# Feed-forward products that read their moving columns in turn from the two halves of a tile

## The chip, the cores and the metric

One Trainium2 chip, one of its cores. The metric is the device time of one execution in microseconds (us); lower is better. The kernel before takes 1040.09 us, the median of three runs from 1039.26 to 1040.59.

## What is computed

The kernel computes linear attention followed by a feed-forward network. The attention (8 batches, 8 heads, 576 tokens, head dimension 64, 128 features) makes the rows `x` of 4608 tokens by 512 features; the network then is

```python
h = x @ w_in                                            # 4608 x 512 times 512 x 2048
g = np.maximum(h, 0.0) + alpha * np.minimum(h, 0.0)     # a leaky relu with a slope for each of the 2048
return (g @ w_out).astype(np.float32)                   # 4608 x 2048 times 2048 x 512
```

Inputs and outputs are float32.

## The kernel before

**Layout.** Tokens lie along the free dimension everywhere in the feed-forward: a tile holds 128 features by 512 tokens, and the output leaves as 512 features by 4608 tokens, which the host transposes. The tokens are nine chunks of 512 (`NC2`, `C2`). The stationary operand of a matmul is a 128x128 block of weights; the moving operand is one tile of 512 columns; the result is one bank of PSUM with 512 columns.

**Three matmuls for one product.** Every operand of the feed-forward is split into a high part, rounded to the type fp32r, and the rest (`rnd` at L139 on ScalarE, `low` at L143 on VectorE). A product of two blocks is three matmuls that add into one bank: high weight by high tokens, low weight by high tokens, high weight by low tokens. They are written out in `gemm1` (L538 to L545), `gemm2` (L550 to L554) and `three` (L828 to L831). The trace shows these operands as f32.

**Stages.** First the attention, 32 pairs of heads, with float32 matmuls: projections (L347), sums of keys and values (L387), denominators (L470, four matmuls that each fill 32 output partitions and read four different moving operands), transposes (L430, L433) and numerators (L452). The weights are unpacked beside it on the other engines. Then the first chunk of tokens with plain products: `up2` calls `gemm1` (16 blocks of 128 rows, 4 parts of the 512 features each), `down2` calls `gemm2` (16 blocks into 4 banks). The first four up products lie between the last attention work. Then the other eight chunks in four pairs, with seven products instead of eight for each 2x2 scheme of blocks (sums and differences of weights and tokens are made beforehand): `unit` calls `product` (L833) for eight units of up products, `down_pair` (L951) does the down products of the pair, 7 times 8 times 2.

**Order.** TensorE, SyncE and GpSimd are issued in the written order throughout (`tc.manual_schedule`); VectorE and ScalarE too in the attention stage, while in the second part the planner of `TileContext`, which simulates a timeline by its own costs, orders them. SyncE's queue carries the loads of weights (`load_up` L621, `load_wv` L923) and some of the loads of tokens (`xr`).

**What goes into the matmuls.** `xs[j]` are the first chunk's tokens, `gh` and `gl` its activated values, `xo[p, n, j]` the tokens of a pair and their sums, `hv[p, k, u]` the activated values of a pair and their sums. All are pairs (high, low) of 128 x 512 views whose columns lie side by side. The last product of the last pair is cut into two pieces of 256 columns (`cuts`), so that its first half leaves while the second is still computed.

Of the kernel before, what the change touches and what calls it, by code (L numbers as in the profile page):

```python
# [20 lines left out]
DM, DFF = 512, 2048  # L21
NP = H // 2
NPAIR = B * NP
NT = B * S
# [7 lines left out]
C2 = 512  # L32
NC2 = NT // C2
# [88 lines left out]
def fused_kernel(ctx: ExitStack, tc: tile.TileContext, kq, v, w_phi, w_in, w_out, alpha, out):  # L122
# [178 lines left out]
    def attention_units(i):  # L301
# [233 lines left out]
        out = [(i + t, u) for t, u in us]  # L535
        return out + first_x(i, lambda: c["r"]) if i < NK else out

    def gemm1(ps, wt, xs, steps=range(NK)):  # L538
        for n in steps:
            j = NK - 1 - n  # L540
            wh, wl = wt(j)
            xh, xl = xs[j]
            pe.matmul(ps, lhsT=wh, rhs=xh, start=n == 0, stop=False)
            pe.matmul(ps, lhsT=wl, rhs=xh, start=False, stop=False)
            pe.matmul(ps, lhsT=wh, rhs=xl, start=False, stop=n == NK - 1)  # L545
# [3 lines left out]

    def gemm2(ps, wt, m, gh, gl, first, last):  # L550
        wh, wl = wt(m)
        pe.matmul(ps, lhsT=wh, rhs=gh, start=first, stop=False)
        pe.matmul(ps, lhsT=wl, rhs=gh, start=False, stop=False)
        pe.matmul(ps, lhsT=wh, rhs=gl, start=False, stop=last)  # L554

    def bank(k, name):
        return (late["psu"] if k else psf).tile([P, C2], F32, tag="fu"[k], name=name)

    xs, po = {}, {}
# [19 lines left out]
    def first_x(j, rows):  # L579
        def cast():  # L580
            xh, xl = (late[n].tile([P, C2], F32R, tag=n, name=f"x0{n}_{j}", bufs=k) for n, k in (("cp", 4), ("pt", 4)))
            rnd(act, xh, rows()[:, :C2])
            xs[0].append((xh, xl))

        def rest():
            xh, xl = xs[0][j]
            low(dve, xl, rows()[:, :C2], xh)

        return [(X0T + j, cast), (X0T + X0L + j, rest)]
# [115 lines left out]
    def up2(c, ff):  # L705
        ps = bank(int(ff >= HEAD), f"h2_{c}_{ff}")
        gemm1(ps, up_plain(ff), xs[c])
        gq[c, ff] = act_g(ps, ff, f"2_{c}_{ff}")
# [6 lines left out]
    def out_tile(m, c):  # L715
        tag, bufs = ("pr", 2) if c % 2 else ("pt", 4)
        return late["pt"].tile([P, C2], F32, tag=tag, name=f"pt{m}_{c}", bufs=bufs)

    def give(m, c, t, cuts=(0, C2), q=None):
        for a, b in zip(cuts, cuts[1:]):  # L720
            (q or nc.sync).dma_start(out[m * P : (m + 1) * P, c * C2 + a : c * C2 + b], t[:, a:b])  # L721
# [3 lines left out]
    def down2(ff):  # L725
        if ff == 0:
            po[0] = [late["pso"].tile([P, C2], F32, tag=f"o{m}", name=f"po0{m}") for m in reversed(range(NK))][::-1]
        gh, gl = gq[0, ff]
        for m in range(NK):
            gemm2(po[0][m], down_plain(ff), m, gh, gl, ff == 0, ff == NF - 1)  # L730
            if ff == NF - 1:
                o = out_tile(m, 0)
                act.copy(o, po[0][m])
                held.append((m, 0, o))
# [4 lines left out]
    xo = {}  # L739
# [3 lines left out]
    def pieces(k):  # L743
        for _ in range(k):
            if prep:
                prep.pop(0)()
# [72 lines left out]
    end = t1 + (len(order) - HEAD) * U2 - 0.002  # L819
# [8 lines left out]
    def three(ps, wh, wl, xh, xl, first, end):  # L828
        pe.matmul(ps, lhsT=wh, rhs=xh, start=first, stop=False, skip_group_check=True)  # L829
        pe.matmul(ps, lhsT=wl, rhs=xh, start=False, stop=False, skip_group_check=True)  # L830
        pe.matmul(ps, lhsT=wh, rhs=xl, start=False, stop=end, skip_group_check=True)  # L831

    def product(ps, p, u, n, first, end):  # L833
        w = wu[p, u, n]
        for j in range(2):
            wh, wl = (w[:, k, j * P : (j + 1) * P] for k in range(2))
            three(ps, wh, wl, *xo[p, n, j], first and j == 0, end and j == 1)

    def copied(ps, name):
        t = late["cp"].tile([P, C2], F32, tag="cp", name=name, bufs=4)  # L840
# [3 lines left out]
    def added(dst, ps, t):  # L844
        dve.tensor_tensor(dst, ps, t, op=ALU.add)  # L845
# [26 lines left out]
    def unit(p, u):  # L872
# [5 lines left out]
        def begin():  # L878
            st["a"] = bank(0, f"pa{tag}")
            product(st["a"], p, u, A11, True, False)  # L880
            st["b"] = bank(1, f"pb{tag}")
            if fresh:
                st["p1"] = copied(st["a"], f"p1_{tag}")
            else:
                act.copy(st["b"], st["a"])

        def second():
            product(st["b"], p, u, A12, fresh, True)

        def rest():  # L890
            g = g4[p, u] = g_tiles(p, u)
            if fresh:
                added(g[0, 0], st["b"], st["p1"])
            leaky(g[0, 0] if fresh else st["b"], g[0, 0], f1, f"11_{tag}")
            product(st["a"], p, u, S2, False, False)
            st["u2"] = copied(st["a"], f"u2_{tag}")
            st["c"] = bank(1, f"pc{tag}")
            product(st["c"], p, u, S1, True, False)
            p5 = copied(st["c"], f"p5_{tag}")
            product(st["a"], p, u, S3, False, False)  # L900
            added(g[1, 1], st["a"], p5)
# [12 lines left out]
    hv, wv = {}, {}  # L914
# [3 lines left out]
    def load_wv(p, k, h):  # L918
        t = late["wv"].tile([P, 2, 2, WN], F32R, tag="wv", name=f"wv{p}_{k}_{h}", bufs=4)
        n = PLACE[ORDER[k]]  # L920
        us = slice(2 * h, 2 * h + 2)
        src = (v_d[us, :, n] if n < 4 else vs_d[us, :, n - 4]).rearrange("u p t c -> p u (t c)")
        nc.sync.dma_start(f(t.rearrange("p u t c -> p u (t c)")), src)  # L923
        wv[p, k, h] = t
# [19 lines left out]
    def some_operand(k=1):  # L944
        for _ in range(k):
            if queue:
                operand(*queue.pop(0))
# [3 lines left out]
    def down_pair(p):  # L951
        c1, c2 = 2 * p - 1, 2 * p
        last_pair = p == NC2 // 2
        bk = {}
        goal = {S1: (2, c2), S2: (0, c2), A12: (0, c1), S3: (2, c2), S4: (0, c2), A22: (2, c1)}
        for k, n in enumerate(ORDER):
            key = {A12: "b", S1: "c", S4: "c"}.get(n, "a")
            if n in (A11, S1):
                for m in range(2):
                    bk[key, m] = late["pso"].tile([P, C2], F32, tag=f"o{'ac'.index(key) * 2 + m}", name=f"q{key}{p}_{m}")  # L960
            um = [(u, m) for u in range(NU) for m in range(2)]
            if last_pair and n == A22:
                um[NU:] = sorted(um[NU:], key=lambda x: x[1])
            turn = 0 if last_pair and n == A22 else 1
            for u, m in um:
                q = 4 * k + u // 2 + 3
                if um.index((u, m)) in (0, 4, 8, 12) and q < 4 * len(ORDER) and (p, *divmod(q, 4)) not in wv:
                    load_wv(p, *divmod(q, 4))
                w = wv[p, k, u // 2][:, u % 2, :, m * P : (m + 1) * P]
                first = n in (A11, S1) and u == 0  # L970
                end = n in (A12, A22, S4) and u == NU - 1
                cuts = (0, C2 // 2, C2) if last_pair and m and n == A22 and u == NU - 1 else (0, C2)
                for a, b in zip(cuts, cuts[1:]):
                    x = [h[:, a:b] for h in hv[p, k, u]]
                    three(bk[key, m][:, a:b], w[:, 0], w[:, 1], *x, first, end)
                yield
                if m == turn and k + u:
                    some_operand()
                    if (k, u) in PIECES:
                        pieces(1)  # L980
                if u == NU - 1:
                    ps = bk[key, m]
                    if n == A11:
                        bk["b", m] = bank(1, f"qb{p}_{m}")
                        act.copy(bk["b", m], ps)
                        continue
                    i = goal[n][0] + m, goal[n][1]
                    if n not in (S3, S4):
                        part[i] = out_tile(*i)
                    x = part[i]  # L990
                    for a, b in zip(cuts, cuts[1:]):
                        if n in (S3, S4):
                            added(x[:, a:b], ps[:, a:b], x[:, a:b])
                        elif len(cuts) > 2 and a:
                            dve.tensor_copy(x[:, a:b], ps[:, a:b])
                        else:
                            act.copy(x[:, a:b], ps[:, a:b])  # L997
                        if n not in (S1, S2):
                            give(*i, x, (a, b), pool if len(cuts) == 2 else act if a else nc.sync)

    with tc.manual_schedule(engines={et.PE, et.SP, et.Pool}):
# [12 lines left out]
        for p in range(1, NC2 // 2 + 1):  # L1014
            more_pairs = p < NC2 // 2
            queue += [(p, k, u) for k in range(len(ORDER)) for u in range(NU)]
            for u in range(NU):
# [31 lines left out]
                if u == NU - 2:  # L1049
                    downs = down_pair(p)  # L1050
# [46 lines left out]
```

## Time and profile before

| | |
|---|---|
| median of three runs | 1040.09 us (1039.26 to 1040.59) |
| span of the profiled execution | 1038.6 us |
| TensorE busy | 1024.7 us, 99% |
| weight loads busy (beside the matmuls) | 799.5 us, 77% |
| VectorE busy | 791.8 us, 76% |
| ScalarE busy | 607.4 us, 58% |
| GpSimd busy | 242.1 us, 23% |
| memory traffic | 258.47 MB, mean 249 GB/s |

The profile is that of one execution. Its names for the engines are PE (TensorE's matmuls), PEld (its weight loads, which run beside them), DVE (VectorE), ACT (ScalarE), POOL (GpSimd) and SP (SyncE). A matmul's time is given with its latency, and matmuls overlap: how often one starts tells the rate, not how long one lasts. PEclk is the granted clock of TensorE, in tenths or as a share of full speed. "L829" is line 829 of the kernel.

### The profile page before, as it was taken

Reading aid. Unit: us, or ns where it says so; the run is one execution under the profiler, and the core shown is the slowest. Engines: PE = TensorE matmul, PEld = TensorE weight load, DVE = VectorE, ACT = ScalarE, POOL = GpSimd, SP = SyncE. Lnnn points to the kernel's source line nnn. Section 1 sums busy time; section 2 is a strip of 40 time slices with the busy share of each in tenths; the row PEclk is TensorE's granted clock in tenths of the full one; section 3 lists DMA queues with packets and bytes.
Section 4 is the critical chain, followed back from the end, with each engine's and each line's share of the span. In section 5 each row is a group of like instructions: output and inputs, shape, how many; then the busy total and the mean of one; then the engine's idle time right before and its main releaser. Section 6 shows DMA issues by size and latency. Waiting matters only on the chain.

```text
span 1038.6 us, 18434 instructions
## 1 busy us (share of the span) xinstructions
PE 1024.7 (99%) x6881; PEld 799.5 (77%) x6881; DVE 791.8 (76%) x1238; ACT 607.4 (58%) x1163; POOL 242.1 (23%) x218
## 2 busy tenths in 40 slices
PE   9999999999999999999999999999999999999998
PEld 6666676666676787787888888888888888888887
DVE  7999999999997677679988365887455877564864
ACT  4787787777877344465565344465444555443553
POOL 0556566565664231212000000000000000000001
PEclk9999999999999999999999999999999999999999
DMA  5678888888883899998668556668556667565564
GB/s 173 233 271 277 295 283 287 305 303 294 288 282 140 324 332 400 364 339 279 229 212 276 186 200 233 223 199 295 190 192 243 213 207 260 169 206 191 174 215 170
DMA packets 99336, 258.47 MB, mean 249 GB/s; under 512 B 12656, under 2 KB 13296, under 8 KB 99248
## 3 DMA queue, kind: packets, MB, share of 16 engines
q1 hardware_dynamic: 88816, 221.71, 62.5%
q0 software_dynamic: 10000, 35.39, 9.0%
q8 instruction: 54, 0.88, 0.3%
q14 instruction: 34, 0.28, 0.1%
q10 hardware_dynamic: 432, 0.20, 0.1%
HBM read 196.16 MB, written 60.96 MB: 248 GB/s over the span
## 4 chain that ended last, share of the span: by engine, by line
PE 79%; DMA 6%; DVE 4%; ACT 1%; issue 1%; SPq 1%; ACTq 0%; DVEq 0%
PE kv L387 5%; PE pa L829 5%; PE pa L831 5%; PE pa L830 5%; PE qa L831 5%; PE qa L829 5%; PE qa L830 5%; PE n L452 5%; PE pj L347 4%; DMA wa<-u_d 4%; PE pc L831 3%; PE pc L830 3%; PE pc L829 3%; PE qc L831 2%; PE qc L829 2%; PE qc L830 2%
## 5 line engine op out<-in xcount | busy, mean ns | idle before, releaser
L139 ACT CAST hv<-g 128x512 fp32r<-128x512 f32 x224 | 137.1, 622 | 100.7 <-DVE hv L143 42.0
L143 DVE TENSOR_TENSOR hv<-g,hv 128x512 fp32r<-128x512 f32 x224 | 152.0, 691 | 54.6 <-ACT hv L139 53.6
L721 POOL DMA_DIRECT2D out_dram<-pt x35 | 18.9, 541 | 527.6 <-ACT pt L997 439.9
L830 PE MATMUL qa<-hv,wv 128*128 128x512 f32 (+1 forms) x257 | 99.8, 388 | 0.0
L831 PE MATMUL qa<-hv,wv 128*128 128x512 f32 (+1 forms) x257 | 99.8, 388 | 0.0
L829 PE MATMUL qa<-hv,wv 128*128 128x512 f32 (+1 forms) x257 | 99.8, 388 | 0.0
L352 DVE TENSOR_TENSOR t<-pj,m 128x1024 f32<-128x1024 f32 (+2 forms) x67 | 78.9, 1177 | 4.4
L351 DVE TENSOR_REDUCE m<-pj 128x8 f32<-128x1024 f32 (+2 forms) x67 | 78.3, 1169 | 4.7 <-PE pj L347 4.7
L347 PEld LDWEIGHTS pj<-w_sb,raw 64*128 64x128 f32 x1024 | 62.5, 187 | 16.9 <-issue 13.7
L200 POOL TENSOR_TENSOR aw<-ew,aw 128x512 f32<-128x512 f32 x32 | 41.1, 1285 | 143.0 <-DVE ew L196 143.0
L347 PE MATMUL pj<-w_sb,raw 64*128 64x128 f32 x1024 | 71.9, 279 | 1.9 <-DVE t L352 1.7
L374 POOL TENSOR_TENSOR y<-xk 128x1024 f32<-128x1024 f32 x30 | 70.9, 2363 | 0.0
L452 PE MATMUL n<-qf,sf 128*64 128x288 f32 x512 | 69.2, 412 | 0.0
L366 ACT ACTIVATE xk<-t 128x1024 f32<-128x1024 f32 (+1 forms) x66 | 66.0, 1080 | 4.4 <-DVE t L352 4.4
L443 ACT ACTIVATE qf<-qt 128x512 f32<-128x512 f32 x128 | 66.8, 637 | 0.0
L849 ACT ACTIVATE r<-g 128x512 f32<-128x512 f32 x65 | 37.6, 625 | 48.6 <-DVE g L845 48.6
L387 PE MATMUL kv<-xk,v 128*64 128x256 f32 x512 | 62.3, 385 | 0.0
L850 DVE SCALAR_TENSOR_TENSOR g<-r,al,g 128x512 f32<-128x512 f32 x65 | 46.3, 749 | 17.9 <-ACT r L849 17.9
L463 ACT COPY s<-n 128x288 f32<-128x288 f32 x64 | 25.2, 398 | 58.4 <-PE n L452 58.4
L139 ACT CAST xo<-xr 128x512 fp32r<-128x512 f32 x56 | 34.1, 622 | 39.3 <-DVE xr L774 19.0
L830 PEld LDWEIGHTS qa<-hv,wv 128*128 128x128 f32 x257 | 48.2, 188 | 10.0
L829 PEld LDWEIGHTS qa<-hv,wv 128*128 128x128 f32 x257 | 48.2, 188 | 10.0
(195 smaller groups left out, 2606.0 us busy)
## 6 DMA issues: line engine op xcount, KB each, us to landing
wv<-vs_d SPq DMA_DIRECT2D x64, 512.0 KB, 3.8
ws<-us_d SPq DMA_DIRECT2D x54, 512.0 KB, 4.5
wv<-v_d SPq DMA_DIRECT2D x48, 512.0 KB, 3.6
wa<-u_d SPq DMA_DIRECT2D x37, 512.0 KB, 6.2
raw<-kq_dram SPq DMA_DIRECT2D x31, 576.0 KB, 5.1
v<-v_dram SPq DMA_DIRECT2D x32, 320.0 KB, 4.1
rr<-rec_d SPq DMA_DIRECT2D x64, 144.0 KB, 3.4
x_d<-rr SPq DMA_DIRECT2D x32, 288.0 KB, 2.6
```

Source lines behind the costliest of these rows:

```text
L139: return act.copy(dst, src)
L143: return eng.tensor_tensor(dst, src, f(hi), op=ALU.subtract)
L347: pe.matmul(dst[h, j], lhsT=c["raw"][hs, ts], rhs=w_sb[hs], start=True, stop=True)
L351: dve.tensor_reduce(m, src, axis=AX.X, op=ALU.max, apply_absolute_value=True)
L352: dve.tensor_tensor(t[:, hs, js], src, m.unsqueeze(3).broadcast_to([P, nh, nj, FD]), op=ALU.subtract)
L374: pool.tensor_tensor(y, x[:, :, : 2 * FD], x[:, :, 2 * FD :], op=ALU.add)
L387: pe.matmul(c["kv"][h * D : (h + 1) * D, 0:2], lhsT=c["v"][:, tp, h, :], rhs=c["x", ch][:, :, h, j, :], start=tp == 0, stop=tp == NV - 1,)
L443: act.activation(c["qf"][:, h, a, : 4 * P], ps.rearrange("p j f -> p (j f)"), AF.Exp, scale=sg)
L452: pe.matmul(ps[h * D : (h + 1) * D, :], lhsT=c["st"][:, a, h * D : (h + 1) * D], rhs=c["qf"][:, h, a, u * HS : (u + 1) * HS], start=a == 0 ...
L829: pe.matmul(ps, lhsT=wh, rhs=xh, start=first, stop=False, skip_group_check=True)
L830: pe.matmul(ps, lhsT=wl, rhs=xh, start=False, stop=False, skip_group_check=True)
L831: pe.matmul(ps, lhsT=wh, rhs=xl, start=False, stop=end, skip_group_check=True)
```

## The change

Each product of the feed-forward gets its moving operand through a view that puts the two halves of the columns side by side: with `fold`, the columns of 512 are taken in the order 0, 256, 1, 257, 2, 258, and so on. Nothing is moved in memory. The columns of the result come out in that order, in the up products and again in the down products, so the output's tokens are permuted within each chunk of 512: after both foldings column 4a + k holds token 128k + a. The host puts them back when it transposes the output. In the cut product at the end the halves are those of the folded order. All elementwise work, the loads, the stores and the attention are as before.

```diff
+    def fold(x):
+        return x.rearrange("p (m n) -> p n m", m=2)
+
     def gemm1(ps, wt, xs, steps=range(NK)):
         for n in steps:
             j = NK - 1 - n
             wh, wl = wt(j)
-            xh, xl = xs[j]
+            xh, xl = map(fold, xs[j])
             pe.matmul(ps, lhsT=wh, rhs=xh, start=n == 0, stop=False)
...
     def gemm2(ps, wt, m, gh, gl, first, last):
         wh, wl = wt(m)
+        gh, gl = fold(gh), fold(gl)
         pe.matmul(ps, lhsT=wh, rhs=gh, start=first, stop=False)
...
             wh, wl = (w[:, k, j * P : (j + 1) * P] for k in range(2))
-            three(ps, wh, wl, *xo[p, n, j], first and j == 0, end and j == 1)
+            three(ps, wh, wl, *map(fold, xo[p, n, j]), first and j == 0, end and j == 1)
...
-                    x = [h[:, a:b] for h in hv[p, k, u]]
+                    x = [fold(h)[:, a // 2 : b // 2] for h in hv[p, k, u]]
                     three(bk[key, m][:, a:b], w[:, 0], w[:, 1], *x, first, end)
...
-    return np.ascontiguousarray(r.results[0]["out_0_dram"].T)
+    o = r.results[0]["out_0_dram"].reshape(DM, NC2, C2 // 4, 4)
+    return np.ascontiguousarray(o.transpose(1, 3, 2, 0).reshape(NT, DM))
```

## Rows read from the trace of the kernel before

**Rows 1.** The page's busy times, and the granted clock in 40 slices.

```profile
PE 1024.7 (99%) x6881; PEld 799.5 (77%) x6881; DVE 791.8 (76%) x1238; ACT 607.4 (58%) x1163; POOL 242.1 (23%) x218
...
PEclk9999999999999999999999999999999999999999
```

**Rows 2.** Busy times by stretch, us; (x) instructions, then clock, DMA share, GB/s.

```profile
core 0: us, PE busy (x) PEld busy (x) DVE busy (x) ACT busy (x) POOL busy (x), PEclk, DMA share, GB/s
342.00:440.00 98.00, 94.47 (x412) 76.66 (x411) 67.99 (x120) 41.22 (x73) 22.00 (x37) 1.00 0.97 365
440.00:500.00 60.00, 58.95 (x261) 48.48 (x260) 49.80 (x88) 34.52 (x62) 10.11 (x20) 1.00 0.87 318
500.00:1035.00 535.00, 534.07 (x2357) 441.59 (x2355) 361.95 (x564) 273.09 (x469) 16.75 (x31) 1.00 0.64 212
```

**Rows 3.** Matmuls in order of time from 639.65 us: start, duration, line.

```profile
639.65 0.39 PE L830 MATMUL pa<-xo,ws 128*128 128x512 f32 x1
639.88 0.39 PE L831 MATMUL pa<-xo,ws 128*128 128x512 f32 x1
640.11 0.39 PE L829 MATMUL pa<-xo,ws 128*128 128x512 f32 x1
640.33 0.39 PE L830 MATMUL pa<-xo,ws 128*128 128x512 f32 x1
```

**Rows 4.** A weight load there in order of time, and the mean of one line's loads.

```profile
640.11 0.19 PEld L830 LDWEIGHTS pa<-xo,ws 128*128 128x128 f32 x1
...
L829 PEld LDWEIGHTS qa<-hv,wv 128*128 128x128 f32 x257 | 48.2, 188 | 10.0
```

**Rows 5.** Matmuls of the attention in order of time; the the second row is the start of the third.

```profile
150.09 1.04 PE L433 MATMUL qt<-ident,t 128*128 128x128 f32 x8
...
155.14 0.43 PE L470 MATMUL d<-qf,sf 128*32 128x288 f32 x4
...
155.14 1.15 PE L470 MATMUL d<-qf,sf 128*32 128x288 f32 x16
```

**Rows 6.** The same two kinds by line: busy us, mean ns of one, idle before.

```profile
L470 PE MATMUL d<-qf,sf 128*32 128x288 f32 x512 | 37.0, 406 | 0.0
L433 PE MATMUL qt<-ident,t 128*128 128x128 f32 x256 | 33.2, 273 | 0.0
```

**Rows 7.** The six pieces of 256 columns at the end, in order of time.

```profile
1033.89 0.28 PE L829 MATMUL qa<-hv,wv 128*128 128x256 f32 x1
...
1034.00 0.28 PE L830 MATMUL qa<-hv,wv 128*128 128x256 f32 x1
...
1034.12 0.28 PE L831 MATMUL qa<-hv,wv 128*128 128x256 f32 x1
...
1034.24 0.28 PE L829 MATMUL qa<-hv,wv 128*128 128x256 f32 x1
```

**Rows 8.** Line 829 alone in the stretches of rows 2: PE, PEld.

```profile
342.00:440.00 98.00, 10.26 (x26) 4.88 (x26) 1.00 0.97 365
440.00:500.00 60.00, 33.62 (x87) 16.20 (x87) 1.00 0.87 318
500.00:1035.00 535.00, 305.18 (x785) 147.31 (x785) 1.00 0.64 212
```

**Rows 9.** Chain of work that ended last, 379 to 440 us: start, us, what.

```profile
379.46 16.13 DMA wa<-u_d
...
401.80 14.13 DMA wa<-u_d
...
428.27 10.48 DMA wa<-u_d
```

**Rows 10.** Line 543, the first up products: durations, first and last start.

```profile
L543 PE MATMUL h<-x0cp,wo x24: 389/391/496, 319.5 to 357.2; 128*128 128x512 f32 x24
```

**Rows 11.** The same chain, 543 to 562 us, and the like place at 697.

```profile
543.89 0.36 SPq L923
...
544.30 7.76 DMA xr<-x_d
...
560.21 0.61 DVE hv L143
...
560.87 0.50 PE qc L831
...
697.15 7.96 DMA xr<-x_d
```

**Rows 12.** All waits of TensorE's matmuls from 520 us on: total, times, longest.

```profile
PE qc L831 <- DVE hv L143: 0.7, 2, 0.4
```

## The prediction

> **What bounds the kernel now.** I read the busy shares first. [...] From 500 to 1035 us, where only products of the feed-forward run, TensorE is busy 534.07 of 535 us with 2357 matmuls: one starts every 535 / 2357 = 0.227 us [rows 2]. From 342 to 500 us it idles 98 - 94.47 + 60 - 58.95 = 4.6 us, and the DMA share there is 0.97 and 0.87 [rows 2]. So the end is set by how fast matmuls follow one another, and before 440 us by transfers too.
>
> The third view is the row of starts: 639.65, 639.88, 640.11, 640.33 and so on, each lasting 0.39 us but starting 0.227 us after the one before, whichever of the three lines issued it [rows 3]. The 0.39 us holds latency; the step counts. [...]
>
> [...]
>
> **The change part by part.** Counting the loops, the change touches 192 matmuls of the first chunk's up products (16 blocks, 4 parts, 3 each), 192 of its down products, 4 pairs x 8 units x 7 products x 6 = 1344 up and 1344 down, and 3 more for the cut at the end: 3075. The trace agrees: line 829 alone, a third of the products in pairs, has 26 + 87 + 785 records [rows 8]. No instruction, wait, DMA or byte is added or removed. Each matmul takes its columns as 0, 256, 1, 257, ... instead of 0, 1, 2, ...; columns come out permuted alike in every bank, so all elementwise work in between is untouched, and the order is undone outside the measured time. So the sum has one unknown: the step of a matmul with this pattern. [...]
>
> [...]
>
> The sum at 10.7 ns. From 500 to 1035 us: 2357 x 0.0107 = 25.2 us. From 440 to 500: 261 x 0.0107 = 2.8. From 342 to 440: 412 matmuls, 4.4 us, of which I count nothing, because the chain there runs through weights that take 16.13, 14.13 and 10.48 us to land at a DMA share of 0.97: a faster TensorE waits for them longer [rows 2, 9]. The 48 matmuls of the first up products, from 319.5 us, lie between attention work: 0.5 us, not counted [rows 10]. Given back: at two places the chain leaves TensorE, from 543.9 to 560.9 us and alike near 697, through a 7.76 us transfer of tokens, casts and VectorE's subtractions, and ends at a product; that path doesn't shorten, and TensorE, which now fills it with 17 / 0.227 = 75 matmuls, would wait 0.8 us more at each: 1.6 us [rows 11]. Today's wait there is 0.7 us in two places [rows 12]. VectorE has 362 busy of 535 us, so it doesn't become the bound elsewhere [rows 2]. Together 25.2 + 2.8 - 1.6 = 26.4 us: a span of 1012.2. The median of the runs, 1040.1, lies 1.5 us above the profiled span of 1038.6, which gives 1013.7, so 1014.
>
> The planner that orders VectorE's and ScalarE's work in the second half may price the new pattern otherwise and order them anew. I count nothing, as TensorE idles 0.9 us in 535; a bad order would cost a few waits of the size seen, 0.4 us each [rows 2, 12].
>
> [...]
>
> **The rivals.** [...]
> [...]
>
> [...]
>
> [...]
>
> [...]
>
> **How the numbers follow.** Forecast (the loss goes, wholly or in part) 0.50, at 1014, own range 1005 (all 3075 x 10.7 ns = 33 us, none given back, and 2 us of spread) to 1031 (a third of the gain). Nothing 0.19; stall paid twice 0.11; two steps per column 0.20. The measurement can tell about 0.2% from no change. Faster 0.50, same 0.19, slower 0.31. The range reaches down to the forecast's end and up over the stall paid twice, to 1085; the fourth case, 0.20, is left out.
>
> **What the profile after would show.** If I am right, the starts in the pairs lie 0.216 us apart, TensorE does some 231 matmuls in 50 us where it did 222, its idle time grows before 440 us and at the two places named, and the weight loads end later relative to the next start. [...] The stage before the first product at 319.5 us must be the same [rows 10]. Wrong would be above all the step from the denominators' four streams to one stream in two halves.

## The result

The changed kernel takes 1014.35 us (median of four runs, 1013.82 to 1015.11) where the kernel before took 1039.99 beside it: a ratio of 0.9759, 95% interval 0.9745 to 0.9772. 1014 was forecast. The profiled execution spans 1012.3 us against 1038.6.

The page's busy times answer to [rows 1]:

```profile
span 1012.3 us, 18434 instructions
...
PE 994.4 (98%) x6881; PEld 804.6 (79%) x6881; DVE 787.8 (78%) x1238; ACT 606.6 (60%) x1163; POOL 242.0 (24%) x218
```

Same instructions, 30.3 us less of busy TensorE, and 4.0 us more of idle TensorE (1012.3 - 994.4 = 17.9 against 13.9): 26.3 us together. The stretches, with the first one ahead of those of [rows 2]:

```profile
319.00:342.00 23.00, 22.20 (x167) 15.61 (x166) 16.96 (x22) 14.69 (x32) 10.46 (x7) 1.00 0.33 120
342.00:440.00 98.00, 93.29 (x421) 79.87 (x420) 68.08 (x124) 42.30 (x76) 21.76 (x37) 0.98 0.99 375
440.00:500.00 60.00, 58.27 (x270) 50.56 (x269) 52.30 (x90) 35.21 (x64) 10.12 (x19) 1.00 0.87 317
500.00:1009.00 509.00, 505.38 (x2339) 440.43 (x2337) 355.68 (x559) 270.52 (x467) 16.82 (x31) 1.00 0.67 221
```

In the last stretch a matmul costs 505.38 / 2339 = 0.2161 us of busy TensorE, where it was 534.07 / 2357 = 0.2266. The starts show it one by one, against the 0.227 of [rows 3]:

```profile
639.83 0.38 PE L833 MATMUL pa<-xo,ws 128*128 128x512 f32 x1
640.05 0.38 PE L834 MATMUL pa<-xo,ws 128*128 128x512 f32 x1
640.27 0.38 PE L835 MATMUL pa<-xo,ws 128*128 128x512 f32 x1
640.48 0.38 PE L833 MATMUL qa<-hv,wv 128*128 128x512 f32 x1
```

640.48 - 639.83 is three steps of 0.217. Had all 3075 matmuls brought the forecast's 10.7 ns, it would be 33 us. Most of what is missing shows in TensorE's waits from 320 us on (who waited for whom: us in total, times, longest):

```profile
PE po L556 <- ACT gh L139: 3.2, 1, 3.2
PE qc L835 <- DVE hv L143: 2.9, 3, 1.3
PE pa L833 <- DVE g L854: 1.7, 1, 1.7
PE pa L833 <- DMA wa<-u_d: 1.4, 1, 1.4
...
```

The second of them was 0.7 us in [rows 12]; the first is in the stretch that waits for transfers, and it has a consequence that I had not reckoned with:

```profile
360.31 0.48 PE L556 MATMUL po<-gh,wd 128*128 128x512 f32 x1 [3.16 <-ACT gh L139]
...
361.73 0.63 PE L557 MATMUL po<-gh,wd 128*128 128x512 f32 x1
362.15 0.63 PE L558 MATMUL po<-gl,wd 128*128 128x512 f32 x1
362.58 0.63 PE L556 MATMUL po<-gh,wd 128*128 128x512 f32 x1
...
362.00:372.00 10.00, 10.00 (x41) 8.49 (x41) 6.94 (x14) 4.20 (x7) 4.81 (x8) 0.86 0.92 306
```

These are the matmuls behind the wait, in order of time, and the row of the stretch after it (columns as in [rows 2]). Behind 3.16 us of idle time the starts lie 0.42 to 0.43 apart from 361.7 to 364.7 us, twice the 0.216 before the wait; the clock granted in these 3 us is 0.50, and 0.86 in the stretch from 362 to 372 us. Seven such steps cost 7 x 0.21 = 1.5 us. In the kernel before, the idle time at this place was 1.4 us and the clock stayed at 1.00:

```profile
PE po L552 <- ACT gh L139: 1.4, 1, 1.4
...
362.00:372.00 10.00, 10.00 (x46) 8.29 (x45) 8.86 (x14) 4.25 (x8) 4.24 (x6) 1.00 0.83 269
```

### The profile page after: what moved, and what is told of

Its sections match the earlier page's. It is cut to its first block, busy times and chain, and to the rows that moved or that the text cites. A ratio compares the mean times of both kernels' runs of the same rounds, so it can differ in the third digit from the quotient of the medians.

```text
span 1012.3 us, 18434 instructions
## 1 busy us (share of the span) xinstructions
PE 994.4 (98%) x6881; PEld 804.6 (79%) x6881; DVE 787.8 (78%) x1238; ACT 606.6 (60%) x1163; POOL 242.0 (24%) x218
## 4 chain that ended last, share of the span: by engine, by line
PE 83%; DVE 4%; DMA 3%; ACT 0%; issue 0%; SPq 0%; ACTq 0%; DVEq 0%
PE kv L387 5%; PE n L452 5%; PE qa L835 5%; PE qa L834 5%; PE qa L833 5%; PE pa L833 5%; PE pa L834 5%; PE pa L835 5%; PE pj L347 4%; PE pc L835 3%; PE pc L834 3%; PE pc L833 3%; PE qc L835 2%; PE d L470 2%; PE qc L833 2%; PE qc L834 2%
## 5 line engine op out<-in xcount | busy, mean ns | idle before, releaser
L835 PE MATMUL qa<-hv,wv 128*128 128x512 f32 (+1 forms) x257 | 97.3, 379 | 0.0
L834 PE MATMUL qa<-hv,wv 128*128 128x512 f32 (+1 forms) x257 | 97.2, 378 | 0.0
L833 PE MATMUL qa<-hv,wv 128*128 128x512 f32 (+1 forms) x257 | 97.2, 378 | 0.0
L347 PEld LDWEIGHTS pj<-w_sb,raw 64*128 64x128 f32 x1024 | 63.2, 190 | 17.5 <-issue 13.9
```

Of the source, the lines that this page charges most:

```text
L347: pe.matmul(dst[h, j], lhsT=c["raw"][hs, ts], rhs=w_sb[hs], start=True, stop=True)
```

## Experiments

### Which orders cost what

The loss is here what reading side by side took longer than the halves in turn, 10.5 ns of 226.6. The first theory, A, the prediction's, was that the loss belongs to one unbroken stream, so that every order that takes no two neighbours one after the other steps at 0.216 us. B is that it takes two or more places far apart, each of which is read on side by side: 0.216 for halves and quarters in turn, and more the wider the gap for a single stream with gaps. The first three kernels below were made to tell A from B, and from a D that is stated with the runs; each gives the first chunk and the four pairs of chunks an order of their own, so that one trace shows five steps. The step is read as a stretch's busy time over its matmuls; each of these kernels ran once. The edits of this part are shown in short, against the changed kernel: `p` is the number of the pair, 0 for the first chunk, and the host's side is left out.

**Strides and quarters.** The first chunk is read in halves, the four pairs in every 2nd, every 4th and every 16th column and in the four quarters in turn; `fold` is, in the four pairs:

```diff
-        return x.rearrange("p (m n) -> p n m", m=2)
+        return x.rearrange("p (m n) -> p n m", m=(2, 256, 128, 32, 4)[p])
```

> [...]

Measured 1519.64 us. The busy times in stretches of the first chunk and the four pairs (span, PE busy and matmuls, clock, DMA share, GB/s):

```profile
385.00:405.00 20.00, 20.00 (x95) 1.00 1.02 408
500.00:700.00 200.00, 200.00 (x444) 1.00 0.39 128
750.00:1000.00 250.00, 250.00 (x544) 1.00 0.34 113
1050.00:1300.00 250.00, 250.00 (x579) 1.00 0.35 118
1330.00:1500.00 170.00, 170.00 (x602) 1.00 0.49 159
```

Every 2nd column 0.450 us, every 4th 0.460, every 16th 0.432, quarters in turn 0.282. Theory A falls at once: none of these orders takes neighbours one after the other, and all are slower than side by side. B falls too as it stood, since a gap of two columns costs as much as one of sixteen, and quarters more than halves.

**Runs.** Runs of 64, 2, 4, 8 and 32 neighbours, taken in turn from the halves:

```diff
-        return x.rearrange("p (m n) -> p n m", m=2)
+        return x.rearrange("p (m n r) -> p n m r", m=2, r=(64, 2, 4, 8, 32)[p])
```

> Runs of neighbouring columns, taken in turn from the two halves: 64 columns in a run in the first chunk, 2, 4, 8 and 32 in the four pairs. Theory A: the longer the unbroken run, the more of the loss is back: between 0.216 and 0.227, rising from 2 to 64, and near 0.227 at 32 and 64. Theory B: 0.216 at all lengths, as both streams are far apart. A rival, D (the loss is one step for every fixed number of columns of a stream, at a border in memory): 0.216 only where a run is shorter than the stretch between borders, and a jump from 0.216 to 0.227 between two of the lengths.

Measured 1147.44 us; the stretches of the four pairs, columns as above:

```profile
500.00:640.00 140.00, 140.00 (x413) 1.00 0.50 168
660.00:810.00 150.00, 150.00 (x601) 1.00 0.61 206
830.00:970.00 140.00, 140.00 (x577) 1.00 0.63 211
990.00:1130.00 140.00, 140.00 (x593) 1.00 0.59 191
```

Runs of 2 take 0.339 us, of 4 0.250, of 8 0.243, of 32 0.236; runs of 64, in the first chunk, 0.227 (49 steps from 387.84 to 398.94 us). None is faster than side by side, and those up to 32 are slower, against A, B and D alike. The alternation of halves is no good in itself: of runs of 1, 2, 4, 8, 32 and 64 columns only single ones brought a gain (0.216).

**Blocks.** The halves of small blocks in turn, which puts the two places 2, 4, 16 or 64 columns apart (128 in the first chunk):

```diff
-        return x.rearrange("p (m n) -> p n m", m=2)
+        return x.rearrange("p (k m n) -> p k n m", m=2, k=(2, 128, 64, 16, 4)[p])
```

> The halves are those of smaller blocks, so the two places read in turn lie 2 columns apart (first pair: 0, 2, 1, 3), 4 apart (second), 16 apart (third), 64 apart (fourth) and 128 apart (first chunk). Theory A: 0.216 for all of them, as no two successive columns are neighbours, but for one in four of the first pair. Theory B: 0.216 for the far ones, 64 and 128 apart, 0.227 for the near ones; where it changes tells how far is far. [...]

Measured 1020.07 us; the four pairs:

```profile
500.00:560.00 60.00, 59.99 (x265) 1.00 0.68 218
580.00:715.00 135.00, 133.64 (x618) 1.00 0.69 233
730.00:860.00 130.00, 129.72 (x601) 1.00 0.70 238
880.00:1000.00 120.00, 120.00 (x558) 1.00 0.62 206
```

Two apart (0, 2, 1, 3): 0.226, nothing gained. Four apart (0, 4, 1, 5, ...): 0.216, the whole gain, as at 16 and 64 apart (0.216, 0.215) and at 128 in the first chunk (0.216, 52 steps from 387.63 to 398.86 us). So from 4 to 256 columns apart the distance made no difference (0.215 to 0.216), and blocks of eight suffice. What does change between blocks of four and of eight is how the order goes through stretches of four neighbouring columns. That gave theory F, a count: an order is taken apart into its 1st, 3rd, 5th column and so on, and its 2nd, 4th, 6th, and what counts is how many columns such a part takes from a stretch before it goes to another. Side by side, the first part is 0, 2, then 4, 6: two from a stretch (0.227). With halves in turn it is 0, 1, 2, 3: four (0.216). With every 2nd column it is 0, 4, 8: one (0.450).

**Places.** The test of F: a second half that begins 2 or 1 columns early (so that the two parts no longer go to another stretch at the same place of the order; F counts four as before), halves in turn with even columns first (two from a stretch), and quarters of blocks of 16.

```diff
-        return x.rearrange("p (m n) -> p n m", m=2)
+        # step and count of each dimension, outermost first, in the first three pairs
+        dims = ([[1, 256], [254, 2]], [[1, 256], [255, 2]], [[1, 2], [2, 128], [256, 2]])[p - 1]
+        return bass.AP(x.tensor, x.offset, [list(x.ap[0])] + dims)
```

> [...] First pair of chunks: the second half begins 2 columns early (0, 254, 1, 255, ...), second pair: 1 column early. [...] Third pair of chunks: halves in turn, even columns first (0, 256, 2, 258, ...). F: 0.227, two from each stretch. A single count of stretches says 0.45 as for every 2nd column. Fourth pair: quarters of blocks of 16 in turn (0, 4, 8, 12, 1, ...): one from a stretch at a time, come back to after four columns. [...] In the first two pairs of chunks the last columns of a tile are left out and others are read twice, and the tokens' order is taken back only for the rest, so the output there isn't the network's.

Measured 1053.93 us; the four pairs:

```profile
500.00:560.00 60.00, 59.72 (x277) 1.00 0.71 240
575.00:710.00 135.00, 133.54 (x618) 1.00 0.70 236
730.00:860.00 130.00, 130.00 (x575) 1.00 0.67 228
880.00:1040.00 160.00, 160.00 (x597) 1.00 0.51 168
```

The shifted halves keep the whole gain (59.72 / 277 = 0.216 and 133.54 / 618 = 0.216), so it doesn't matter whether both parts change at the same place. Even columns first: 0.226, as F said, where a count over both parts together said 0.45. The near quarters take 0.268, better than one column of four without return (0.43 to 0.46) and near the far quarters' 0.282.

| order | columns that a part takes from four neighbours at a time | us per matmul |
|---|---|---|
| halves in turn, also shifted by 1 or 2; halves of blocks of 8, 32, 128 | 4 | 0.215 to 0.216 |
| side by side; halves of blocks of 4; halves in turn, even columns first | 2 | 0.226 to 0.227 |
| quarters in turn, far and near | 1, come back to after four columns | 0.282, 0.268 |
| runs of 2 from the halves | 1, come back to after four columns | 0.339 |
| every 2nd, 4th, 16th column | 1, not come back to soon | 0.450, 0.460, 0.432 |
| runs of 4, 8, 32, 64 from the halves | 2 | 0.250, 0.243, 0.236, 0.227 |

F orders all rows but the last. It is a count made on the orders; how TensorE reads them no row shows. Open is what coming back costs (0.268 to 0.339 for orders that F puts together), and why runs of 4, 8 and 32 take 0.250, 0.243 and 0.236 where F counts two columns a stretch and says 0.227; no kernel here took that apart.

### Where the first chunk's part went

**Only the pairs.** The first chunk is read side by side again:

```diff
-            xh, xl = map(fold, xs[j])
+            xh, xl = xs[j]
...
-        gh, gl = fold(gh), fold(gl)
```

> Only the four pairs read in turn from the halves; the first chunk reads its columns side by side as before. If the first chunk is bound by its transfers, its 384 matmuls gain nothing: 1014 us, within 0.2% of the whole change, and the clock doesn't fall in that stretch. If its gain counts in full, 384 x 10.9 ns = 4.2 us are missing: 1018.5 us.

Measured 1015.06 us (1014.11 to 1018.67), ratio 0.9781, interval 0.9762 to 0.98. It overlaps that of the whole change, but holds 1018.5 too (0.9798 of the 1039.51 beside it), so the times alone don't decide. The profiled executions, as far as one of each can tell, show no gain from the first chunk's 384 matmuls: both span 1012.3 us, and by 440 us this kernel has done 164 + 424 matmuls from 319 us on, the full change 167 + 421. The clock is full in its stretch (columns as in [rows 2]):

```profile
342.00:440.00 98.00, 95.67 (x424) 79.19 (x423) 68.68 (x124) 42.74 (x77) 21.77 (x37) 1.00 0.99 375
```

**The wait taken away.** In the changed kernel a cast of weight sums stands on ScalarE ahead of the activation that TensorE's product needs, and waits for its buffer's transfer (ScalarE in order of time):

```profile
357.61 0.62 ACT L139 CAST sv<-sv 128x512 fp32r<-128x512 f32 x1 [3.80 <-DMA v_d<-raww]
358.13 0.59 ACT L258 ACTIVATE r<-h 128x512 f32<-128x512 f32 x1
359.64 0.62 ACT L139 CAST gh<-g 128x512 fp32r<-128x512 f32 x1 [0.92 <-DVE g L262]
```

```diff
-            todo.append((max(t1 + 0.0002, t1 + (SUM0 + SUMD * n + dt) * U2 + 0.002), parts[k]))
+            todo.append((max(t1 + 0.0002, t1 + (SUM0 + SUMD * n + dt + 2 * (n == 1 and k in ("half1", "store1"))) * U2 + 0.002), parts[k]))
```

> The changed kernel, with the cast that waits 3.8 us for a buffer at 357 us put two thirds of a block pair later. If the 3.2 us wait of TensorE behind it and the half clock after it (12 matmuls at 0.425 instead of 0.216, 1.6 us with those before) are what the first chunk's gain went into, both go: 1014.35 - 4.8 = 1009.5 us. If the transfers set the pace of the whole stretch, the next landing takes the wait's place: 1014, the same within 0.2%.

Measured 1014.29 us, ratio 0.9759, interval 0.9743 to 0.9776: the same. The edit did what it should, as the stretch's row and TensorE's waits from 320 us on show:

```profile
342.00:440.00 98.00, 92.36 (x422) 78.62 (x421) 68.58 (x124) 42.24 (x76) 21.73 (x37) 1.00 1.00 378
...
PE pa L833 <- DMA wa<-u_d: 3.3, 2, 1.9
...
PE po L556 <- ACT gh L139: 1.2, 1, 1.2
```

The wait of 3.2 us is gone, one of 1.2 us stands at 379 us instead, and the clock stayed at 1.00; but TensorE now waits 3.3 us for landings of weights where it was 1.4, and has done 422 matmuls by 440 us instead of 421. So what the wait gives back goes to landings, at a DMA share of 1.00: the transfers set the pace.

**All those sums later.**

```diff
-SUM0, SUMD = 1.5, 3.0
+SUM0, SUMD = 2.5, 3.0
```

> The changed kernel with all sums of weights of the first stretch one block later, their loads, casts and stores too. The same two theories: 1009.5 us if the one wait is the cause, 1014 if the transfers set the pace; above 1014 if the stores of sums that come later delay the loads of them in the first pair.

Measured 1014.71 us, ratio 0.9769, interval 0.9752 to 0.9787: the same again, with 423 matmuls from 342 to 440 us. The wait at 357 us is gone here too; one of 1.7 us stands at 380 us, and a lower clock behind it, 0.84 from 382 to 392 us.

### The waits that the faster products bring to light

**The next pair's tokens earlier.**

```diff
-PIECES = [(k, u) for k in range(1, 7) for u in range(NU)][4 : 4 + 48 : 3]
+PIECES = [(k, u) for k in range(1, 7) for u in range(NU)][2 : 2 + 48 : 3]
```

> The changed kernel with the pieces of the next pair's tokens taken two steps earlier in the down products. If the path from the tokens' transfer through casts and subtractions is what holds TensorE for 2.9 us in three places, most of it goes: 1011.5 us. If those pieces only wait for their buffers or take VectorE's time from other work, 1014 within 0.2%.

Measured 1010.77 us (1009.84 to 1011.52), ratio 0.9728, interval 0.9713 to 0.9743: faster than the change, though narrowly: its interval begins where this one ends. TensorE's wait for VectorE in the pairs went from 2.9 us in three places to one of 0.6, which is 2.3 of the 3.6 us:

```profile
PE qc L835 <- DVE hv L143: 0.6, 1, 0.6
```

**The same without the change**, the same line in the kernel before:

> The kernel before, with only the next pair's tokens taken two steps earlier. If the 2.9 us that this saves behind the change is a wait that the faster products brought to light, there is next to nothing to gain here, where TensorE waits 0.7 us at that place: 1039.4 us, the same within 0.2%. If the earlier pieces are worth as much without the change, 1036.4 us.

Measured 1039.14 us, ratio 1.0009, interval 1.0000 to 1.0019: nothing gained, though the waits of [rows 12] are gone. So the 3.6 us are not a gain that lay there already: the faster products lengthened the waits, and the earlier pieces shorten them.

**Four steps earlier** (`[0 : 0 + 48 : 3]`):

> The changed kernel with those pieces four steps earlier instead of two. If two steps already removed what was to be had (0.6 us of the wait left), 1010.3 us, the same as with two; if the earlier loads now wait for the buffers of the pair before and hold SyncE's queue of weights, above 1012 us.

Measured 1011.35 us, ratio 0.9741, interval 0.9727 to 0.9756: not to be told from two steps, nor by its interval from the change. The fastest version is the change with the pieces two steps earlier, 2.7% faster than the kernel before.

## Why the prediction was right, and where it was not

**The bound.** Right: TensorE's steps set the end from 500 us on, and a step that is 10.5 ns shorter shortened that part nearly by its count.

**The step.** No run shows the 10.7 ns by which the sum lets a step fall; they were the author's estimate. The runs showed 10.5 ns in their place: 534.07 / 2357 = 0.2266 us before, 505.38 / 2339 = 0.2161 after. No order here took less than 0.215. Steps of about twice that do come, with other orders: 0.432 to 0.460 for the strides.

**The reason for the choice** was only half right. The denominators' groups of four matmuls, with four operands, take (1.15 - 0.43) / 3 = 0.240 us for 4 x 288 columns [rows 5], about twice as many columns per us as a matmul of the feed-forward. From that I concluded that jumping between places is cheap and that the loss belongs to an unbroken stream, which two halves split. Jumping is not cheap: quarters take 0.282, runs of 2 0.339 and every 2nd column 0.450. Nor is the loss due to the stream being unbroken: blocks of four break it and gain nothing (0.226). The orders that gain, halves of a tile or of blocks from eight columns up, are those where F counts four columns of a stretch. Four separate matmuls in [rows 5] could not show that: that the forecast's step came nearly true was in part luck. The chance of 0.20 for two steps per column was fair for a conclusion with that gap.

**The loss is not a fixed one of each matmul**: only weakly supported by the 256-column pieces, whose starts lie 0.11 to 0.12 us apart [rows 7], but right, for with the same weight loads the order of reading alone moved the step between 0.215 and 0.460 us.

**The terms of the sum**, in matmuls ahead of the kernel before, at 0.216 us each:

| stretch | forecast | measured |
|---|---|---|
| to 440 us | 0 | (167 - 164) + (421 - 412) = 12 matmuls, 2.6 us |
| 440 to 500 us | 2.8 us | 9 matmuls, 1.9 us |
| from 500 us | 25.2 - 1.6 = 23.6 us | 26.3 - 2.6 - 1.9 = 21.8 us |

(164 is the kernel before's count from 319 to 342 us.) The 12 matmuls of the first row need not come from the change. The kernel before with the earlier pieces, in which no product is folded and whose edit lies in the pairs' down products, behind this stretch, has done 164 + 422 by 440 us in its profiled execution, 10 more than the kernel before in its own:

```profile
342.00:440.00 98.00, 96.07 (x422) 78.65 (x421) 67.95 (x122) 42.56 (x76) 21.72 (x37) 1.00 0.98 369
```

With the pairs alone it is 164 + 424. So two executions without a folded product differ by 2 us in this stretch, and nothing here contradicts the forecast of no gain from it. The last term is short by 1.8 us: the step fell by 10.5 ns and not 10.7 (0.5 us), and 2.2 us more of waiting for VectorE came back instead of 1.6, in three places rather than two (0.6 us); the rest isn't taken apart. That 1014 came out within 1 us is partly luck: misses of about 2 us cancel.

**What I did not see**: the wait of 3.2 us in the first chunk and the half clock behind it. They cost nothing that the times show when they are taken away, because transfers set the pace there.

**The rivals.** Two steps per column, a step about twice as long, did not come with this order: it is 0.216 us, and 0.432 to 0.460 came with the strides alone. A stall paid twice would have made the step longer than 0.227, and it became shorter. "Nothing" falls with the order alone having moved the step, while a weight load took 188 ns before and 189 after.

## What to carry to other kernels

Where matmuls follow each other without idle time, measure the step between their starts for more than one order of reading; here 10.5 ns of 227, 5%, were lost in how the moving operand was read. For these f32 operands of 512 columns, an order that takes single columns in turn from two places, each read on side by side, took 0.216 us instead of 0.227, while strides took 0.432 to 0.460; halves of blocks of eight columns (0.216) do as well as halves of a tile, so the permutation can be kept small. When the bound engine gets faster, look for the waits that were just hidden before: moving the tokens' loads was worth nothing with the old order and 3.6 us with the new.

## What the runs showed of the hardware that I had not expected

Every 2nd column is as dear as every 4th (0.450 and 0.460 us), although two of them lie among four neighbours, and every 16th is a little cheaper (0.432). Both are read from rows; the first agrees with the count F, one column of four at a time in both; for the second F has no reason.

TensorE's clock fell to 0.50 for 3 us after 3.16 us of idle time in the changed kernel and stayed at 1.00 after 1.2 us with the pairs alone, but the length of the wait alone does not order the runs. It fell after 2.3 us in the run with the pieces two steps earlier (0.92 from 362 to 372 us) and after 1.7 us in the run with all sums later (0.84 from 382 to 392 us), and not after 1.9 us in the kernel before with the earlier pieces (the last two of these runs follow in that order, each with the matmul behind the wait and the stretch after it):

```profile
380.49 0.48 PE L556 MATMUL po<-gh,wd 128*128 128x512 f32 x1 [1.69 <-ACT gh L139]
382.00:392.00 10.00, 10.00 (x40) 8.45 (x40) 7.60 (x14) 4.11 (x7) 3.09 (x6) 0.84 1.02 395
...
360.49 0.50 PE L552 MATMUL po<-gh,wd 128*128 128x512 f32 x1 [1.86 <-ACT gh L139]
362.00:372.00 10.00, 10.00 (x45) 8.26 (x44) 7.96 (x14) 4.21 (x7) 5.04 (x8) 1.00 0.95 330
```

No run here was made to find what decides.
